# Two late second-layer tiles in halves, other PSUM banks for the last results, and the last inverse deviations one by one

## The chip, the cores and the metric

The kernel runs on one core of one Trainium2 chip. The metric is the device time of one execution in microseconds, as the median of several runs. A core has five engines that work side by side, each through its own list of instructions in order: TensorE (PE, matmuls and transposes), VectorE (DVE), ScalarE (ACT), GpSimd (POOL), and SyncE (SP), which here only issues DMAs. An instruction that waits holds up everything behind it on its own engine.

## The reference

Two stages. A retention layer without a softmax (8 batches, 8 heads, 576 positions, 64 wide), and a feed-forward layer over its 4608 rows of 512:

```python
scores = (q @ k.T) / 8 * gamma_h ** (i - j)      # for i >= j, else 0; one gamma per head
x = concat_heads(scores @ v)                     # 4608 x 512
h = x @ w_in                                     # 4608 x 1024
e = exp(h - max(h)); sm = e / sum(e)
u = h * sm
ln = (u - mean(u)) / sqrt(var(u) + 1e-6) * g_ln
out = ln @ w_out                                 # 4608 x 512
```

## The kernel before

The 4608 rows are 36 tiles of 128, and two neighbouring tiles form a window of 256 positions. The retention part is also cut into 36 steps (a window times four heads, two steps to a window). The program is one list per engine, written out by hand in `ORDER` (lines 53 to 110): each engine runs its names in that order. A planner (`plan`, `order_ops`) only merges the five lists into one order in which tiles are handed out; it moves nothing within an engine. The names, with a number for the tile or the step:

- SP: `ldq`, `ldk`, `ldv` load the inputs (one DMA each, four for the steps 16, 17, 34 and 35); `lx` is a DMA transpose of a tile's product (L568); `out` stores a result.
- POOL: `sq`, `sk`, `cv` scale and cast q, k and v; `sm`, `sc` carry the state between windows; `rs` works out the inverse deviations of both tiles of a window (`rstd`, L770: an addition, then a power, on 128x2).
- TensorE: `T` transposes q and k (L519), `S` scores (L620), `I` and `V` the retention output (L580), `K` the state; `M1` is the first layer of a tile (L713: 8 matmuls into the two banks of "h"), `M2` the second (L786: 8 matmuls of 128x128 by 128x512 into one bank). `L35` is the one late transpose that TensorE makes (L531). The last tile's second layer is cut into two halves of columns, `M2_35` and `M3`.
- ACT: `Te` copies the transposed q and k out of the bank (L550), `xe` the retention output (L702), `ex` is the exponential with its sum (L721), `va` the sum of squares of some tiles (L750), `fx` squares the sums (L759), `Le` copies L's result (L548), `oe` scales a tile's result by its inverse deviation on the way out of PSUM (L795; `oz` for M3).
- DVE: `mask` applies the decay mask (L656), `so` the product h*e (L736, L731), `bnA` and `bnB` the statistics of its halves (L742, with an aggregate, L744), `fin` the deviation's argument for tiles with `va`; `cnt`, `cs`, `ci` count the rows whose sums are in range.

For a tile t the chain is: M1 (bank "h"), ex, so, then lx (or L), then M2 six tiles behind, then oe and out. M1 of the next tile needs "h" back, so it waits for so. M2 waits for the transposed product and for a bank; oe waits for M2 and for rs of its window.

PSUM has eight banks: "xy", "s" and "h" of two banks each with one tile in flight, and "tl" with two banks for the transposes of q and k. Once the last of these has been copied out, "tl" is closed and its two banks become the pool "o2", two tiles of one bank (`bank`, L488). Which pool a tile's M2 writes to is said by `home` (L136); the constant `OT` is the first tile in "o2". Scores use "s" as well, so an M2 in "s" stands between two steps' scores, and the next score waits until oe has emptied it. Results in SBUF ("osb") have three buffers.

The end of TensorE's list before, and those of ACT and SP:

```python
PE:  ... V33 T35 S34 M1_31 M2_27 I34 V34 S35 M1_32 M2_28 I35 V35 M1_33 M2_29 M2_30 M1_34 M2_31 M2_32 M1_35 M2_33 L35 cs M2_34 M2_35 M3
ACT: ... oe26 Te35 xe33 ex31 oe27 xe34 ex32 fx14 oe28 va31 fx15 ex33 va30 xe35 oe30 ex34 oe29 fx16 oe31 ex35 oe32 fx17 oe33 Le35 oe34 oe35 oz
SP:  ... ldk35 lx26 ldq35 out23 lx27 out24 ldv34 lx28 ldv35 out25 lx29 lx30 out27 out26 lx31 lx32 out28 lx33 out30 out29 lx34 out31 ...
```

Of the kernel before, what the change touches and what calls it, by code (L numbers as in the profile page):

```python
# [13 lines left out]
P = 128  # L14
# [3 lines left out]
for _b in range(0, B, 4):  # L18
# [25 lines left out]
R0 = 9  # L44
OT = 30
SPL = ()
# [7 lines left out]
    PE=(  # L54
# [10 lines left out]
    ),  # L65
    ACT=(
# [9 lines left out]
    ),  # L76
    DVE=(
# [9 lines left out]
    ),  # L87
# [9 lines left out]
    ),  # L97
# [38 lines left out]
def home(t):  # L136
    return "h" if t == NT - 1 else "o2" if t >= OT else "xy" if late(t) and t % 2 else "s"


def late(t):  # L140
    return t + LAG >= 37
# [7 lines left out]
def plan():  # L149
# [49 lines left out]
    for t in range(NT):  # L199
# [11 lines left out]
        if c:  # L211
            op(f"fx{w}", "ACT", "fx", [f"ex{t - 1}", f"ex{t}"], (m + 1, 2.6))
            if va:
                op(f"fin{w}", "DVE", "fin", [f"fx{w}", f"va{t - 1}", f"va{t}"], (m + 1, 4.3))
            op(f"rs{w}", "POOL", "rs" if va else "rsB", [f"fin{w}"] if va else [f"fx{w}", f"bnB{t - 1}", f"bnB{t}"], (m + 2, 0.0))
        jn = ev_L(t)[:2] == "TL"
        early = t < NJ - 4
        if t in LX:
            op(f"lx{t}", "SP", "lx", [f"so{t}"], (m + 2, 0.1), [("evl", [f"M2_{t}"])], DUR["ltx"])
        lasts = [x for x in range(NT) if NJ - 4 <= x < OT and ev_L(x)[:2] == "Le"]  # L220
# [10 lines left out]
        if t == OT:  # L231
            need += [ev_T(max(x for x in range(NS) if x not in TX)), ev_L(max(x for x in range(OT) if x not in LX))]
        op(f"M2_{t}", "PE", "M2h" if end else "M2", need, (t + LAG, 3.1), [(home(t), [f"oe{t}"])])
        op(f"oe{t}", "ACT", "oeh" if end else "oe", [f"M2_{t}", f"rs{w}"], (t + LAG + 1, 0.1), [("osb", [f"out{t}"])])
        if end:
# [143 lines left out]
def kernel(  # L379
# [381 lines left out]
    def final(w):  # L761
        d = ws[w]
        d["x2"] = pools["sml"].tile([P, 2], FP, tag="w2", name="w2")
        for c in range(2):
# [3 lines left out]
            )  # L768

    def rstd(w):  # L770
        d = ws[w]
        if 2 * w not in VA:
            d["x2"] = pools["sml"].tile([P, 2], FP, tag="w2", name="w2")
            nc.gpsimd.tensor_tensor(out=d["x2"], in0=d["mv"][:, :, 1], in1=d["x"], op=ALU.add)
        d["rs"] = pools["sml"].tile([P, 2], FP, tag="rs", name="rs")
        nc.gpsimd.tensor_tensor(out=d["rs"], in0=d["x2"], in1=small[:, 69:70].to_broadcast([P, 2]), op=ALU.pow)  # L776


    def mm2(t, half=0):
        d = tk[t]  # L780
        nm = "xy" if half else home(t)
        mm = slice(256 * half, 256 * half + (256 if t == NT - 1 else DM))
        o = bank() if nm == "o2" else pools[nm].tile([P, 2, 512], FP, tag=nm, name="o_ps")[:, 0]
        d["o", half] = o = o[:, 0 : mm.stop - mm.start]
        for c in range(8):
            nc.tensor.matmul(  # L786
                out=o, lhsT=d["ev"][:, d["lo"] + c], rhs=w2c16[:, c, mm], start=(c == 0), stop=(c == 7)
            )

    def o_ev(t, half=0):  # L790
        d = tk[t]
        if not half:
            d["osb"] = pools["osb"].tile([P, DM], FP, tag="osb", name="o_sb")
        mm = slice(256 * half, 256 * half + (256 if t == NT - 1 else DM))
        nc.scalar.activation(  # L795
            out=d["osb"][:, mm], in_=d["o", half], func=ACT.Copy, scale=ws[t // 2]["rs"][:, t % 2 : t % 2 + 1]
        )
# [77 lines left out]
    def emit(o):  # L875
# [39 lines left out]
        elif k_ == "cs":  # L915
            count_b()
        elif k_ == "ci":
            nc.vector.tensor_copy(out=count, in_=cur["cs"][0:1, 0:1])
        elif name[:2] == "wi":
            w_in_cast(int(name[2]), name[3] == "b", copy)  # L920
        else:
            dict(
                T=qk_tp, L=ln_tp, K=kv_mm, I=inter, st=state, sc=state_cast, sm=state_next, S=scores, mask=mask, V=av, xe=x_ev, M1_=mm1,
                ex=exp_, so=solu, va=squares, fx=sums2, fin=final, rs=rstd, M2_=mm2, oe=o_ev, out=store, wc=w2_center,
                M=lambda _: mm2(NT - 1, 1), oz=lambda _: o_ev(NT - 1, 1), G=lambda _: g_tp(), WM=lambda _: w2_sum(), wm=lambda _: w2_mean(),
            )[k_](x)
# [155 lines left out]
```

## Time and profile before

| | us |
|---|---|
| median of three runs | 210.21 (209.46 to 211.24) |
| the profiled execution, its own time | 208.5 |
| its span, first to last instruction | 206.7 |
| TensorE busy in the span | 195.5 |
| DVE busy | 151.4 |
| ACT busy | 140.7 |
| POOL busy | 140.2 |

The profile is one execution on the chip. A row of its timeline gives the start in the span, the length, the engine, the line of the kernel, the operation, the tile written and those read, and how many instructions were merged; in brackets stands how long the engine was idle before it and what ended that. A matmul's row is longer than its share of the engine, since matmuls overlap: the distance from one start to the next tells what a group costs. The granted clock of TensorE is 1.000 over the span. The DMA engines' busy share is over nine tenths in many of the slices up to three quarters of the span, and varies behind that.

### The profile page before, as it was taken

How to read it: one execution, taken by the hardware profiler on the slowest of the kernel's cores; microseconds unless marked ns; L12 is line 12 of the kernel's file. 1: busy time of each engine (PE TensorE's matmuls, PEld its weight loads, DVE VectorE, ACT ScalarE, POOL GpSimd, SP SyncE). 2: the span in 40 equal slices, each digit the busy share in tenths (PEclk: the TensorE clock that was granted, in tenths of full speed). 3: DMA queues.
4: the chain of work that ended last, by engine and by line, in shares of the span. 5: the costliest groups of instructions: out<-in, count | busy, mean ns of one | idle time of the engine just before them, and what ended most of it. 6: DMA issues, size and time to landing. Idle time of an engine off the chain costs nothing. (4 is left out here: it accounts for less than half of the span.)

```text
span 206.7 us, 8546 instructions
## 1 busy us (share of the span) xinstructions
PE 195.5 (95%) x3576; PEld 108.3 (52%) x3576; DVE 151.4 (73%) x269; ACT 140.7 (68%) x250; POOL 140.2 (68%) x235
## 2 busy tenths in 40 slices
PE   7996989999999999999999999999999999999981
PEld 2442654665665555555555555565555555544450
DVE  6575779995988878688897857896878685725850
ACT  2375798897776667667866687696868756576451
POOL 7434758999997797987678888789795853121110
PEclk9999999999999999999999999999999999999999
DMA  6999999999977869999999999999989557998734
GB/s 175 344 358 331 327 318 292 294 263 290 244 220 222 248 197 306 228 284 219 265 291 174 221 296 239 217 255 227 326 132 280 124 117 201 165 236 212 115 149 103
DMA packets 91112, 49.12 MB, mean 238 GB/s; under 512 B 29624, under 2 KB 84928, under 8 KB 91072
## 3 DMA queue, kind: packets, MB, share of 16 engines
q1 hardware_dynamic: 90832, 48.38, 96.3%
q8 instruction: 28, 0.46, 1.0%
q10 hardware_dynamic: 240, 0.18, 0.4%
q14 instruction: 12, 0.10, 0.2%
HBM read 32.56 MB, written 9.44 MB: 203 GB/s over the span
## 5 line engine op out<-in xcount | busy, mean ns | idle before, releaser
L713 PE MATMUL h_ps<-w_in,xT 128*128 128x512 f16 x288 | 68.4, 380 | 0.2 <-DVE solu L736 0.2
L786 PE MATMUL o_ps<-w2c,ev 128*128 128x512 f16 (+1 forms) x296 | 67.6, 373 | 0.0
L721 ACT ACTIVATE e_sb<-h_ps 128x1024 f32<-128x1024 f32 x36 | 36.8, 1022 | 23.7 <-PE h_ps L713 17.3
L656 DVE TENSOR_TENSOR ret<-s_ps,masks 128x1024 f16<-128x1024 f32 x36 | 43.9, 1219 | 11.2 <-PE s_ps L620 10.7
L786 PEld LDWEIGHTS <-ev 128*128 128x128 f16 x296 | 28.9, 98 | 33.0
L713 PEld LDWEIGHTS <-xT 128*128 128x128 f16 x288 | 25.4, 98 | 29.3 <-ACT xT L702 0.7
L477 POOL TENSOR_TENSOR q<-rawq,small 128x512 f16<-128x512 f32 x34 | 35.3, 1042 | 7.3 <-DMA rawq<-in_q_dram 6.6
L736 DVE TENSOR_TENSOR solu<-h_ps,e_sb 128x1024 f16<-128x1024 f32 x22 | 26.9, 1224 | 18.0 <-ACT e_sb L721 17.8
L477 POOL TENSOR_TENSOR k<-rawk,small 128x512 f16<-128x512 f32 x34 | 35.3, 1042 | 6.3 <-DMA rawk<-in_k_dram 5.9
L795 ACT ACTIVATE o_sb<-o_ps,rs 128x512 f32<-128x512 f32 (+1 forms) x37 | 25.0, 675 | 19.3 <-PE o_ps L786 7.7
L742 DVE BATCH_NORM_STATS2 bs<-solu 128x6 f32<-128x512 f16 x44 | 29.8, 681 | 0.1
L702 ACT CAST xT<-xy 128x512 f16<-128x512 f32 x36 | 26.5, 736 | 2.8 <-PE xy L580 2.7
L697 POOL CAST sbd<-gg 64x256 f16<-64x256 f32 x64 | 25.4, 397 | 2.5
L482 POOL CAST v<-rawv 128x512 f16<-128x512 f32 x28 | 17.0, 610 | 9.9 <-DMA rawv<-in_v_dram 3.9
L731 DVE SCALAR_TENSOR_TENSOR solu<-h_ps,e_sb 128x1024 f16<-128x1024 f32 x14 | 17.1, 1221 | 5.7 <-ACT e_sb L721 5.6
L550 ACT COPY ev<-tl 128x512 f32<-128x512 f32 (+1 forms) x26 | 17.8, 684 | 2.0 <-PE tl L519 1.8
L688 POOL TENSOR_TENSOR gg<-gt,small 128x128 f32<-128x128 f32 x32 | 13.1, 408 | 7.9 <-DVE gt L683 7.5
L776 POOL TENSOR_TENSOR rs<-w,small 128x2 f32<-128x2 f32 x18 | 12.4, 690 | 8.5 <-DVE w L765 7.5
L750 ACT ACTIVATE junk<-solu,su 128x1024 bf16<-128x1024 f16 x14 | 16.1, 1150 | 0.0
L620 PE MATMUL s_ps<-ev 64*64 64x128 f16 x576 | 15.1, 220 | 0.4 <-ACT o_sb L795 0.2
L580 PE MATMUL xy<-ret,v 64*64 64x128 f16 x576 | 14.9, 220 | 0.0
L580 PEld LDWEIGHTS <-sbd 128*128 128x128 f16 x128 | 9.4, 98 | 9.4 <-issue 1.1
(73 smaller groups left out, 204.6 us busy)
## 6 DMA issues: line engine op xcount, KB each, us to landing
rawq<-in_q_dram SPq DMA_DIRECT2D x32, 256.0 KB, 5.0
rawk<-in_k_dram SPq DMA_DIRECT2D x32, 256.0 KB, 5.5
rawv<-in_v_dram SPq DMA_DIRECT2D x32, 256.0 KB, 5.1
out_dram<-o_sb SPq DMA_DIRECT2D x32, 256.0 KB, 3.6
wst<-in_moe_w_in_dram SPq DMA_DIRECT2D x4, 512.0 KB, 6.9
wst<-in_moe_w_out_dram SPq DMA_DIRECT2D x4, 512.0 KB, 7.4
rawk<-in_k_dram SPq DMA_DIRECT2D x16, 64.0 KB, 3.4
rawv<-in_v_dram SPq DMA_DIRECT2D x16, 64.0 KB, 3.5
```

The source lines that it names most:

```text
L477: eng.tensor_tensor(out=t.rearrange("p j h d -> p h j d"), in0=st[i]["r" + nm], in1=g, op=ALU.mult)
L550: nc.scalar.copy(out=t[:, lo:hi].rearrange("p x (r w) -> p r x w", r=2), in_=tls[n].rearrange("p r x w -> p (r x w)").bitcast(FP).rearrang ...
L580: nc.tensor.matmul(start=(c, e) not in begun, stop=False, skip_group_check=True, **kw)
L656: nc.vector.tensor_tensor(out=d["ret"].rearrange("p e h j q -> p (e h) (j q)")[:, :, 0:n], in0=d["s"].rearrange("p e h j q -> p (e h) (j q ...
L697: nc.gpsimd.tensor_copy(out=t[ee[e], :, :, ee[e]], in_=st[i]["gg"][ee[e]])
L702: nc.scalar.copy(out=xT[:, 2 * w : 2 * w + 2, 2 * hf : 2 * hf + 2].rearrange("p c h (q j) -> p c h j q", j=2), in_=xys[i][:, :, 0:256].rea ...
L713: nc.tensor.matmul(out=h_ps[:, hh], lhsT=xT[:, t, dc], rhs=w_in16[:, dc, hh], start=(dc == 0), stop=(dc == 3),)
L721: nc.scalar.activation(out=d["e"], in_=d["h"], func=ACT.Exp, accum_out=se[:, t : t + 1])
L736: nc.vector.tensor_tensor(out=d["solu"], in0=d["h"], in1=d["e"], op=ALU.mult)
L742: nc.vector.bn_stats(out=d["bs"][:, half], in_=d["solu"][:, half * 512 : half * 512 + 512])
L786: nc.tensor.matmul(out=o, lhsT=d["ev"][:, d["lo"] + c], rhs=w2c16[:, c, mm], start=(c == 0), stop=(c == 7))
L795: nc.scalar.activation(out=d["osb"][:, mm], in_=d["o", half], func=ACT.Copy, scale=ws[t // 2]["rs"][:, t % 2 : t % 2 + 1])
```

## The change

- `CUT = (29, 32)`: the second layer of tiles 29 and 32 is issued in two groups of four matmuls, `M2_t` and `N_t`, into one accumulation. The first layer of tiles 33 and 35 stands between them. oe and the buffer of the transposed product now wait for `N_t`.
- Banks: `OT` goes from 30 to 27, so the M2 of tiles 27 to 30, 32 and 33 write to "o2"; those of 31 and 34 write to "s". Before, tiles up to 29 were in "s" and 30 to 34 in "o2". The last tile stays in "h".
- The last window's inverse deviations are worked out one tile at a time: `ra` for tile 34 from its own statistics, then `rs17` for tile 35, each on 128x1. oe34 waits for `ra`.
- Orders: on ACT va31 goes ahead of ex32, xe35 ahead of ex33, and oe29 and oe30 change places. On DVE bnB32 goes ahead of so34. On POOL `ra` comes ahead of rs17. On SP ldq35 goes ahead of lx26, and out30 behind out29 and lx34.

```diff
-OT = 30
+OT = 27
+CUT = (29, 32)
...
-PE:  ... I35 V35 M1_33 M2_29 M2_30 M1_34 M2_31 M2_32 M1_35 M2_33 L35 cs M2_34 M2_35 M3
+PE:  ... I35 V35 M2_29 M1_33 N29 M2_30 M1_34 M2_31 M2_32 M1_35 N32 M2_33 L35 cs M2_34 M2_35 M3
-ACT: ... xe34 ex32 fx14 oe28 va31 fx15 ex33 va30 xe35 oe30 ex34 oe29 fx16 oe31 ex35 ...
+ACT: ... xe34 va31 ex32 fx14 oe28 xe35 fx15 ex33 va30 oe29 ex34 oe30 fx16 oe31 ex35 ...
-DVE: ... so33 bnA32 fin15 bnA33 so34 bnB32 bnB33 bnA34 ...
+DVE: ... so33 bnA32 fin15 bnA33 bnB32 so34 bnB33 bnA34 ...
-POOL: ... rs14 rs15 rs16 rs17
+POOL: ... rs14 rs15 rs16 ra rs17
-SP:  ... ldk35 lx26 ldq35 out23 ... out28 lx33 out30 out29 lx34 out31 ...
+SP:  ... ldk35 ldq35 lx26 out23 ... out28 lx33 out29 lx34 out30 out31 ...
...
-    return "h" if t == NT - 1 else "o2" if t >= OT else "xy" if late(t) and t % 2 else "s"
+    return "h" if t == NT - 1 else "s" if t in (NT - 5, NT - 2) else "o2" if t >= OT else "xy" if late(t) and t % 2 else "s"
...
+    def rstd_of(c):
+        d = ws[NW - 1]
+        y = pools["sml"].tile([P, 1], FP, tag=f"wy{c}", name="w2")
+        nc.gpsimd.tensor_tensor(out=y, in0=d["mv"][:, c, 1:2], in1=d["x"][:, c : c + 1], op=ALU.add)
+        d["rs", c] = pools["sml"].tile([P, 1], FP, tag=f"rs{c}", name="rs")
+        nc.gpsimd.tensor_tensor(out=d["rs", c], in0=y, in1=small[:, 69:70], op=ALU.pow)
...
-        for c in range(8):
+        for c in range(4 if t in CUT else 8):
             nc.tensor.matmul(
                 out=o, lhsT=d["ev"][:, d["lo"] + c], rhs=w2c16[:, c, mm], start=(c == 0), stop=(c == 7)
             )
+
+    def mm2_rest(t):
+        d = tk[t]
+        for c in range(4, 8):
+            nc.tensor.matmul(
+                out=d["o", 0], lhsT=d["ev"][:, d["lo"] + c], rhs=w2c16[:, c], start=False, stop=(c == 7)
+            )
```

(The five order lists are shown by their ends, one line each; in the kernel they are strings over several lines.)

More of the change, by code (lines that the diff above doesn't have):

```diff
@@ L54 @@
     PE=(
[10 rows of a table removed]
+        "G T0 S0 K0 K1 T1 I0 S1 V0 I1 V1 M1_0 K2 T2 T3 K3 S2 M1_1 I2 S3 V2 L0 I3 V3 T4 L1 K4 S4 M1_2 K6 WM K5 M1_3 T5 K7  T6 I4 S5 V4 T7 I5 S6 V5 T8 M1_4 I6 S7 V6 K8 T9 L2 M2_0 I7 L3 V7 K9 S8 M1_5 M2_1 I8 L4 T10 V8 S9 K10 M1_6 M2_2  I9 V9 L5 T11 S10 K11 M1_7 M2_3 I10 V10 L6 T12 K12 S11 M1_8 M2_4 I11 V11 L7 T13 K13 S12 M1_9 M2_5 I12 V12 L8 T14  K14 S13 M1_10 M2_6 I13 V13 L9 T15 K15 S14 M1_11 M2_7 I14 V14 T16 S15 M1_12 M2_8 I15 V15 T17 S16 M1_13 M2_9 I16  V16 T18 K18 S17 M1_14 M2_10 I17 T19 V17 K19 S18 M1_15 M2_11 I18 V18 K20 T20 S19 M1_16 M2_12 I19 V19 K21 T21 S20  M1_17 M2_13 I20 V20 T22 K22 S21 M1_18 M2_14 I21 V21 K23 T23 S22 M1_19 M2_15 I22 T24 V22 K24 S23 M1_20 M2_16 I23  V23 K25 T25 S24 M1_21 M2_17 I24 V24 K26 T26 S25 M1_22 M2_18 I25 V25 K27 T27 S26 M1_23 M2_19 I26 V26 K28 T28 S27  M1_24 M2_20 I27 T29 V27 K29 S28 M1_25 M2_21 I28 V28 T30 K30 S29 M1_26 M2_22 I29 T31 V29 K31 S30 M1_27 M2_23 I30  V30 K32 T32 S31 M1_28 M2_24 I31 V31 T33 K33 S32 M1_29 M2_25 I32 T34 V32 S33 M1_30 M2_26 I33 V33 T35 S34 M1_31  M2_27 I34 V34 S35 M1_32 M2_28 I35 V35 M2_29 M1_33 N29 M2_30 M1_34 M2_31 M2_32 M1_35 N32 M2_33 L35 cs M2_34 M2_35 M3"
@@ L65 @@
     ),
     ACT=(
[9 rows of a table removed]
+        "cv0 cv1 Te0 Te1 wi2a wi1a xe0 wi0a wi3a xe1 cv2 ex0 Te2 cv3 Te3 wg4 wg0 ex1 xe2 cv4 Le0 xe3 Te4 Le1 wg6 wg2 cv6  ex2 cv5 va1 cv7 ex3 Te5 va2 Te6 xe4 fx1 fx0 Te7 xe5 va0 Te8 ex4 xe6 Le2 va3 oe0 xe7 Le3 Te9 ex5 oe1 TL8 xe8 ex6  oe2 TL9 xe9 ex7 oe3 xe10 TL10 fx2 ex8 oe4 TL11 xe11 ex9 oe5 fx3 xe12 TL12 fx4 ex10 oe6 xe13 TL13 ex11 oe7 xe14  Te16 ex12 oe8 xe15 Te17 fx5 ex13 oe9 Te18 xe16 ex14 fx6 oe10 va14 xe17 ex15 Te19 oe11 fx7 va15 xe18 ex16 Te20  oe12 xe19 Te21 ex17 oe13 fx8 xe20 Te22 ex18 oe14 xe21 Te23 ex19 oe15 Te24 xe22 va19 ex20 oe16 xe23 Te25 va18  ex21 fx9 oe17 fx10 xe24 Te26 ex22 oe18 xe25 Te27 va22 ex23 fx11 oe19 Te28 xe26 ex24 oe20 va23 xe27 ex25 Te29  oe21 fx12 Te30 xe28 ex26 oe22 Te31 xe29 va26 ex27 oe23 Te32 xe30 ex28 fx13 oe24 va27 xe31 Te33 ex29 oe25 xe32  ex30 Te34 oe26 Te35 xe33 ex31 oe27 xe34 va31 ex32 fx14 oe28 xe35 fx15 ex33 va30 oe29 ex34 oe30 fx16 oe31 ex35  oe32 fx17 oe33 Le35 oe34 oe35 oz"
@@ L76 @@
     ),
     DVE=(
[9 rows of a table removed]
+        "gc sq0 sq1 st0 mask0 st1 wi1b mask1 wi2b wi3b wi0b sk2 sk3 st2 so0 st3 wg5 mask2 mask3 so1 st4 wg7 wg1 wg3  mask4 st6 so2 st5 wc4 wc0 wc7 wc1 st7 so3 mask5 wc5 wc2 wc6 mask6 wc3 mask7 fin0 st8 so4 mask8 st9 bnA4 so5  fin1 bnA5 mask9 st10 bnB4 so6 bnB5 mask10 st11 bnA6 so7 bnA7 mask11 st12 bnB7 so8 bnA8 mask12 st13 bnB6 so9  bnB8 mask13 st14 so10 bnA9 mask14 bnB9 st15 so11 bnA10 mask15 so12 bnA11 mask16 bnB11 bnB10 so13 mask17 st18  bnA13 so14 bnA12 mask18 st19 bnB13 so15 mask19 bnB12 st20 fin7 so16 bnA16 mask20 st21 bnB16 so17 mask21 st22  so18 bnA17 mask22 bnB17 st23 so19 mask23 st24 so20 mask24 bnA20 st25 so21 fin9 mask25 st26 bnB20 so22 bnA21  mask26 st27 bnB21 so23 mask27 st28 so24 bnA24 mask28 bnB24 st29 fin11 so25 mask29 bnA25 st30 so26 mask30 st31  bnB25 so27 mask31 st32 so28 mask32 st33 bnA28 so29 fin13 mask33 bnA29 so30 mask34 bnB29 so31 mask35 bnB28 so32  so33 bnA32 fin15 bnA33 bnB32 so34 bnB33 bnA34 bnB34 so35 cnt bnA35 bnB35 ci"
@@ L214, in plan @@
                 op(f"fin{w}", "DVE", "fin", [f"fx{w}", f"va{t - 1}", f"va{t}"], (m + 1, 4.3))
+            if w == NW - 1:
+                op("ra", "POOL", "rsB", [f"fx{w}", f"bnB{t - 1}"], (m + 2, 0.0))
             op(f"rs{w}", "POOL", "rs" if va else "rsB", [f"fin{w}"] if va else [f"fx{w}", f"bnB{t - 1}", f"bnB{t}"], (m + 2, 0.0))
@@ L218, in plan @@
         if t in LX:
-            op(f"lx{t}", "SP", "lx", [f"so{t}"], (m + 2, 0.1), [("evl", [f"M2_{t}"])], DUR["ltx"])
+            op(f"lx{t}", "SP", "lx", [f"so{t}"], (m + 2, 0.1), [("evl", [f"N{t}" if t in CUT else f"M2_{t}"])], DUR["ltx"])
         lasts = [x for x in range(NT) if NJ - 4 <= x < OT and ev_L(x)[:2] == "Le"]
@@ L232, in plan @@
             need += [ev_T(max(x for x in range(NS) if x not in TX)), ev_L(max(x for x in range(OT) if x not in LX))]
-        op(f"M2_{t}", "PE", "M2h" if end else "M2", need, (t + LAG, 3.1), [(home(t), [f"oe{t}"])])
-        op(f"oe{t}", "ACT", "oeh" if end else "oe", [f"M2_{t}", f"rs{w}"], (t + LAG + 1, 0.1), [("osb", [f"out{t}"])])
+        cut = t in CUT
+        op(f"M2_{t}", "PE", "M2h" if end or cut else "M2", need, (t + LAG, 3.1), [(home(t), [f"oe{t}"])])
+        if cut:
+            op(f"N{t}", "PE", "M2h", [f"M2_{t}"], (t + LAG, 4.0))
+        op(f"oe{t}", "ACT", "oeh" if end else "oe", [f"N{t}" if cut else f"M2_{t}", "ra" if t == NT - 2 else f"rs{w}"], (t + LAG + 1, 0.1), [("osb", [f"out{t}"])])
         if end:
@@ L768, in final @@
             )
+    def rstd_of(c):
[4 more added lines that the diff above has]
+        nc.gpsimd.tensor_tensor(out=d["rs", c], in0=y, in1=small[:, 69:70], op=ALU.pow)
     def rstd(w):
         d = ws[w]
+        if w == NW - 1:
+            return rstd_of(1)
         if 2 * w not in VA:
@@ L795, in o_ev @@
         nc.scalar.activation(
-            out=d["osb"][:, mm], in_=d["o", half], func=ACT.Copy, scale=ws[t // 2]["rs"][:, t % 2 : t % 2 + 1]
+            out=d["osb"][:, mm], in_=d["o", half], func=ACT.Copy,
+            scale=ws[t // 2]["rs", t % 2] if t // 2 == NW - 1 else ws[t // 2]["rs"][:, t % 2 : t % 2 + 1],
         )
@@ L924, in emit @@
                 ex=exp_, so=solu, va=squares, fx=sums2, fin=final, rs=rstd, M2_=mm2, oe=o_ev, out=store, wc=w2_center,
-                M=lambda _: mm2(NT - 1, 1), oz=lambda _: o_ev(NT - 1, 1), G=lambda _: g_tp(), WM=lambda _: w2_sum(), wm=lambda _: w2_mean(),
+                M=lambda _: mm2(NT - 1, 1), N=mm2_rest, ra=lambda _: rstd_of(0), oz=lambda _: o_ev(NT - 1, 1), G=lambda _: g_tp(), WM=lambda _: w2_sum(), wm=lambda _: w2_mean(),
             )[k_](x)
```

34 rows, old and new, of tables (ACT, DVE, PE, POOL) are left out of this document.

## The prediction

> **What bounds the kernel now.** I read the page first (busy shares), then TensorE's timeline over the last 40 us for its idle time, then the SP queue and the landing of its DMAs, then ACT and DVE around each gap.
>
> ```profile
> span 206.7 us, 8546 instructions
> ## 1 busy us (share of the span) xinstructions
> PE 195.5 (95%) x3576; PEld 108.3 (52%) x3576; DVE 151.4 (73%) x269; ACT 140.7 (68%) x250; POOL 140.2 (68%) x235
> ```
>
> TensorE is busy for 95% of the span. Whatever the change can win is idle time of TensorE, and the diff only touches the last eight tiles. So the whole possible gain is in the gaps that the timeline shows there:
>
> ```profile
> 170.61 1.89 PE L786 MATMUL o_ps<-w2c,ev 128*128 128x512 f16 x8
> ...
> 173.36 0.32 PE L519 MATMUL tl<-ident,q 64*64 64x64 f16 x16 [0.29 <-POOL q L477]
> ...
> 173.67 0.42 PE L620 MATMUL s_ps<-ev 64*64 64x128 f16 x16
> ...
> 178.42 0.42 PE L620 MATMUL s_ps<-ev 64*64 64x128 f16 x16 [0.20 <-ACT o_sb L795]
> ```
>
> By the order list these are M2_26 (170.61), T35 (0.29 idle, waiting for sq35 on POOL), S34, and S35 (0.20 idle, waiting for oe27 to free the bank "s"). Then the end:
>
> ```profile
> 183.13 1.89 PE L713 MATMUL h_ps<-w_in,xT 128*128 128x512 f16 x8 [0.15 <-DVE solu L736]
> 184.86 3.62 PE L786 MATMUL o_ps<-w2c,ev 128*128 128x512 f16 x16
> 188.31 1.89 PE L713 MATMUL h_ps<-w_in,xT 128*128 128x512 f16 x8
> 190.04 3.62 PE L786 MATMUL o_ps<-w2c,ev 128*128 128x512 f16 x16
> 193.49 1.89 PE L713 MATMUL h_ps<-w_in,xT 128*128 128x512 f16 x8
> 195.22 1.89 PE L786 MATMUL o_ps<-w2c,ev 128*128 128x512 f16 x8
> 197.85 0.62 PE L531 MATMUL o_ps<-ident,solu 128*128 128x128 f16 x8 [0.74 <-ACT o_sb L795]
> 198.40 0.19 PE L873 MATMUL cs<-small,cn 128*1 128x1 f32 x2
> 198.52 3.65 PE L786 MATMUL o_ps<-w2c,ev 128*128 128x512 f16 x24
> ```
>
> These are M1_33, M2_29 with M2_30, M1_34, M2_31 with M2_32, M1_35, M2_33, L35, cs, and M2_34, M2_35 and M3. A group of eight matmuls takes 1.73 us from start to start (193.49 to 195.22), four take 0.865. The reader should see two kinds of stretch. Between M1_33 and M1_34 there are three groups (5.18 us) and no gap: TensorE is the bound. Between M1_35 and L35 there are only two (3.46), and L35 comes 4.36 after M1_35 started. That 4.36 is a chain through other engines: exp on ACT, the product on DVE, then the next user of the bank "h" or of the product. It is the least distance of one first-layer tile from the next. So the end is a PE-bound part with surplus work between two tiles, followed by a chain-bound part with too little.
>
> **The change part by part.**
>
> 1. *Two groups.* M2_29 and M2_32 are cut in halves: the first half of M2_29 goes ahead of M1_33, the second behind it, and likewise around M1_35. From the start of M1_33 to L35, TensorE then has 3 first-layer tiles (5.19), halves of M2_29, M2_32 and again M2_32 (2.60) and M2_30, M2_31, M2_33 (5.19): 12.98 us, with 2.6 us between any two tiles. The chain needs 3 x 4.36 = 13.08. The two nearly meet, and I take the longer. Before it was 197.85 - 183.13 = 14.72. That is 1.64 less, but half a tile (0.865) now stands ahead of M1_33: 0.77 gained. The 0.15 before M1_33 goes too, as M2_29 fills it. The number of matmuls is the same, and a group that pauses keeps its bank, so I put nothing on the cut; were each cut to cost one matmul more (0.22), it would be 0.4.
>
> 2. *Banks.* M2_27 to M2_29 move from "s" to the pair "o2"; M2_31 and M2_34 move from "o2" to "s". S35 no longer waits for oe27: 0.20 gained. M2_34 no longer waits for oe33. The price: M2_27 is now the first to take the banks of "tl", free when Te35 has read them. Its row is the copy on ACT just behind oe26:
>
> ```profile
> 172.93 0.69 ACT L795 ACTIVATE o_sb<-o_ps,rs 128x512 f32<-128x512 f32 x1 [0.53 <-DMA out_dram<-o_sb]
> ...
> 178.28 0.73 ACT L702 CAST xT<-xy 128x512 f16<-128x512 f32 x1
> 180.71 1.02 ACT L721 ACTIVATE e_sb<-h_ps 128x1024 f32<-128x1024 f32 x1 [1.70 <-DVE bs L742]
> ...
> 183.57 1.14 ACT L750 ACTIVATE junk<-solu,su 128x1024 bf16<-128x1024 f16 x1
> ...
> 200.69 1.16 ACT L795 ACTIVATE o_sb<-o_ps,rs 128x512 f32<-128x512 f32 x2 [1.61 <-POOL rs L776]
> 202.26 0.47 ACT L795 ACTIVATE o_sb<-o_ps,rs 128x256 f32<-128x256 f32 x1 [0.41 <-PEq L1037]
> ```
>
> oe26 ends at 173.62 and Te35 follows within a microsecond, while M2_27 comes a whole first-layer tile (1.73) after S34's end: hidden.
>
> 3. *ACT.* va31 (1.14, the size of va30's row at 183.57) moves into the 1.70 of idle time before ex32 (180.71), behind xe34 (178.28): hidden; without that room it would delay ex32 and so M1_33 by what sticks out. xe35 goes ahead of ex33, which waits for M1_33 anyway. oe29 and oe30 change places to follow the order of M2.
>
> 4. *DVE.* bnB32 goes ahead of so34.
>
> ```profile
> 181.85 1.23 DVE L736 TENSOR_TENSOR solu<-h_ps,e_sb 128x1024 f16<-128x1024 f32 x1 [0.90 <-ACT e_sb L721]
> 186.20 1.22 DVE L736 TENSOR_TENSOR solu<-h_ps,e_sb 128x1024 f16<-128x1024 f32 x1 [3.12 <-ACT e_sb L721]
> 187.34 0.68 DVE L742 BATCH_NORM_STATS2 bs<-solu 128x6 f32<-128x512 f16 x1
> ```
>
> Between the end of one product and the start of the next there are 4.36 - 1.22 = 3.14 us. It now holds three statistics (3 x 0.68), fin15 and an aggregate; if the last two take as long as one statistic together, that is 2.7, and 0.4 is left. If they took double, so34 would be 0.3 late, and with it L35. I take nothing.
>
> 5. *POOL, last inverse deviations.* Tile 34's is worked out by itself (ra) before tile 35's. The rows at 200.69 and 202.26 show what this is worth: oe34 waited for POOL until 200.69, though M2_34 ended near 200.4, but the last output oz waits for M3 (198.52 + 3.65 = 202.17), not for oe34. So it gains nothing at the end, and out34 leaves some 0.3 sooner. Two small POOL operations more cost at most the same 0.4 that oz has to spare.
>
> 6. *SP queue.* This is the part that speaks against the change. ldq35 (four issues) now goes ahead of lx26, the DMA transpose that M2_26 reads.
>
> ```profile
> 166.12 1.23 SPq L568 DMA_TRANSPOSE ev<-solu  x1
> 167.45 1.96 SPq L467 DMA_DIRECT2D rawq<-in_q_dram  x4
> 169.51 1.32 SPq L806 DMA_DIRECT2D out_dram<-o_sb  x1
> ...
> 179.50 2.65 SPq L568 DMA_TRANSPOSE ev<-solu  x2
> ```
>
> lx26 went out at 166.12. Behind four loads that hold the queue from 167.45 to 169.51 (2.06) it goes out at 168.18. From issue to landing, the last ten transposes (from 161 us on, so far as the trace holds their landing) took, as minimum, median and maximum:
>
> ```profile
> DMA to landing us min/median/max: 3.1/3.5/4.1
> ```
>
> So lx26 lands at 171.28, 171.68 or 172.28, and M2_26, which started at 170.61 with no wait, is late by 0.67, 1.07 or 1.67. Behind it on TensorE stand I33, V33, T35, S34, M1_31. Of this, 0.29 comes back at T35: ldq35 leaves 1.33 sooner, so sq35 is there first. The rest, 0.38, 0.78 or 1.38, stays in TensorE's order. oe26 is 0.69 long and follows M2_26, so S34 (three small stages later) finds its bank free. Loads, lx27 and all later ones keep their places: the two exchanged lengths cancel.
>
> 7. *M2_29 earlier.* It could start at 182.98 (the end of V35: 183.13 less 0.15) less 0.20 for S35 = 182.78, plus the delay of step 6: 183.16, 183.56 or 184.16. But lx29, the first of the pair at 179.50, has this row of its own:
>
> ```profile
> DMA to landing us min/median/max: 4.1/4.1/4.1
> ```
>
> It lands at 183.6. Before, M2_29 came at 184.86 and did not see it; now it does. M2_29 starts at the later of the two: 183.6 in the low and middle cases, 184.16 in the high one. This wait therefore hides most of what step 6 does.
>
> *Later transposes.* lx33 and lx34 leave when so33 and so34 are done. M2_34 comes 4.36 + 0.67 after so34, above the 4.1 maximum, so nothing.
>
> *Sum.* L35 starts at M2_29 + 0.865 + 13.08 = 183.6 + 13.945 = 197.55, against 197.85. Everything behind L35 (M2_34, M2_35, M3, oz, out35) keeps its distances. The span is 0.30 shorter: 206.4. That execution took 208.5 beside its span of 206.7, so the sum is 208.2 against 208.5. It was quicker than all three runs (median 210.21), so I carry over the difference, not the level: 209.9.
>
> **The rivals.**
>
> *All gaps close (faster).* If lx26 and lx29 land in time, M2_29 starts at 182.78, L35 at 196.73, 1.12 earlier: 209.1. It needs lx26 within 2.4 us of its issue (170.61 - 168.18) and lx29 within 3.3 (182.78 - 179.50); no transpose in the window was under 3.1. [...]
>
> *A late transpose decides (slower).* One mechanism: lx26 behind the loads. Break-even is M2_29 at 197.85 - 13.945 = 183.91, which is lx26 landing 3.85 us after its issue. All 25 transposes of the trace spread further than the last ten:
>
> ```profile
> DMA to landing us min/median/max: 3.1/4.2/6.6
> ```
>
> At their median of 4.2, M2_26 is 1.77 late, M2_29 starts at 184.26, and the kernel is 0.35 slower: 210.6. At 6.6 it is 2.75 slower: 213.0. For it: lx26 now stands behind eight loads in a row (ldk35's four and ldq35's). Against: it stood behind ldk35's four before, and the last ten transposes kept within 4.1.
>
> *It does nothing at the end.* If a link of the chain is longer than 4.36 in the new order (step 4, or the cut), L35 keeps its 197.85 whatever happens ahead of it: 210.2.
>
> **How the numbers follow.** 0.56 for the forecast (M2_29 between 183.16 and 184.16: 209.5 to 210.5), 0.14 for all gaps closing, 0.24 for a late transpose (about 0.04 of it beyond 2.1 us), 0.06 for nothing at the end. No case reaches 1% faster (2.1 us), as all the gaps that are touched sum to 1.12 once the half tile is paid; 1% is about what a measurement of this kernel can tell from no change, as its three runs alone spread from 209.46 to 211.24. For that spread I leave 0.06 to faster and 0.06 to slower, 0.88 to within 1%. The range takes the fast rival's 209.1 and the slow one's 210.6, and widens each by 0.4 and 0.8, the first for the spread of a median, the second also for the tail towards 213: 208.7 to 211.4.
>
> **What would show it.** In the trace after: M2_26 with an idle time of 0.7 to 1.7 before it; no idle time before T35 and S35; M2_29's first four matmuls waiting for a transpose until about 183.6; M1_33 to L35 in 13.1 us instead of 14.72; L35 with little idle time before it; oe34 not waiting for POOL. It is wrong if M2_26 does not wait (step 6), if M1_33 to L35 stays above 13.6 (step 1), or if something outside these eight tiles moves.

## The result, and the profile after

| | us |
|---|---|
| kernel before, median of 15 runs | 209.52 (208.59 to 211.24) |
| changed kernel, median of 15 runs | 207.95 (206.86 to 210.28) |
| ratio of the two kernels' runs (their medians alone give 0.9925) | 0.993, 95% interval 0.9905 to 0.9956 |
| profiled execution of the changed kernel, its own time and span | 209.56 and 207.8 |

The change makes the kernel faster by 0.7% (0.9 to 2.0 us). It is within 1%, as forecast, but outside the range of 208.7 to 211.4, and five times the 0.3 us forecast. The profile that came with it shows the opposite at first sight: its span is longer than that of before.

```profile
span 207.8 us, 8550 instructions
## 1 busy us (share of the span) xinstructions
PE 196.0 (94%) x3576; PEld 108.1 (52%) x3576; DVE 152.1 (73%) x269; ACT 139.9 (67%) x250; POOL 140.9 (68%) x237
```

So this execution is one of the slowest of the fifteen (only one run, 210.28, which the ratio leaves out, took longer than its 209.56), while the profiled one of before, at 208.5, was under the fastest of its fifteen (208.59). TensorE's timeline of the changed kernel, from M2_26 on:

```profile
173.07 1.90 PE L776 MATMUL o_ps<-w2c,ev 128*128 128x512 f16 x8 [1.34 <-DMA ev<-solu]
174.81 0.39 PE L561 MATMUL xy<-ev,sbd 128*128 128x128 f16 x4
175.13 0.42 PE L561 MATMUL xy<-ret,v 64*64 64x128 f16 x16
175.38 0.29 PE L500 MATMUL tl<-ident,q 64*64 64x64 f16 x16
...
179.94 0.42 PE L561 MATMUL xy<-ret,v 64*64 64x128 f16 x16
180.19 0.39 PE L601 MATMUL s_ps<-ev 64*64 64x128 f16 x16
...
184.65 1.04 PE L776 MATMUL o_ps<-w2c,ev 128*128 128x512 f16 x4
185.53 1.89 PE L694 MATMUL h_ps<-w_in,xT 128*128 128x512 f16 x8
...
198.58 0.62 PE L512 MATMUL o_ps<-ident,solu 128*128 128x128 f16 x8
199.13 0.19 PE L871 MATMUL cs<-small,cn 128*1 128x1 f32 x2
199.25 1.90 PE L776 MATMUL o_ps<-w2c,ev 128*128 128x512 f16 x8
201.45 1.92 PE L776 MATMUL o_ps<-w2c,ev 128*128 128x256 f16 x16 [0.30 <-ACT ev L529]
```

M2_26 is idle for 1.34 us, waiting for its transpose (step 6). T35 and S35 no longer wait. From M1_33 (185.53) to L35 (198.58) it takes 13.05 us instead of 14.72, as step 1 worked out (13.08). New is the last row: M2_35 waits 0.30 for Le35. ACT's timeline shows why:

```profile
200.24 0.69 ACT L792 ACTIVATE o_sb<-o_ps,rs 128x512 f32<-128x512 f32 x1 [2.30 <-DMA out_dram<-o_sb]
200.82 0.58 ACT L529 COPY ev<-o_ps 128x512 f32<-128x512 f32 x1
```

The first is oe33. It waits for the landing of out30 (issued at 195.5, landed 4.6 us later), whose buffer in SBUF it reuses (three buffers), and Le35 stands behind it on ACT.

### The profile page after: what moved, and what is told of

The parts are those of the page before. It is cut to its first block, busy times and chain, and to the rows that moved or that the text cites. A ratio compares the mean times of both kernels' runs of the same rounds, so it can differ in the third digit from the quotient of the medians.

```text
span 207.8 us, 8550 instructions
## 1 busy us (share of the span) xinstructions
PE 196.0 (94%) x3576; PEld 108.1 (52%) x3576; DVE 152.1 (73%) x269; ACT 139.9 (67%) x250; POOL 140.9 (68%) x237
## 5 line engine op out<-in xcount | busy, mean ns | idle before, releaser
L776 PE MATMUL o_ps<-w2c,ev 128*128 128x512 f16 (+1 forms) x288 | 66.2, 373 | 1.6 <-DMA ev<-solu 1.3
L776 PEld LDWEIGHTS <-ev 128*128 128x128 f16 x288 | 27.8, 98 | 34.0 <-DMA ev<-solu 1.8
L766 POOL TENSOR_TENSOR rs<-w,small 128x2 f32<-128x2 f32 x17 | 11.7, 691 | 8.9 <-DVE w L746 7.9
L969 PE MATMUL tl<-zeros 128*128 128x512 f16 x41 | 13.1, 455 | 1.3 <-DVE zeros L932 1.3
```

What stands on the lines that cost most here:

```text
L776: nc.tensor.matmul(out=o, lhsT=d["ev"][:, d["lo"] + c], rhs=w2c16[:, c, mm], start=(c == 0), stop=(c == 7))
```

## The experiments

Between one profile and the next the start of M1_30 moves by up to 2 us (168.87 before, 170.77 in E4) for reasons far ahead of the change: in the first profile of the changed kernel M1_12 already starts 1.02 later than in that of the kernel before (83.61 against 82.59), and M1_30 0.97 later. So each profile below is read from there: the distance from M1_30's start to L35's, and from L35 to the end of the last matmul. "lx26 ahead" is the time from the issue of lx26 to M1_30's start; M2_26 can start 1.74 after M1_30 (170.61 and 168.87 before, where it did not wait).

| kernel | ratio to before (interval) | M1_30 to L35 | L35 to last matmul's end | lx26 ahead |
|---|---|---|---|---|
| before | 1 | 28.98 | 4.31 | 2.75 |
| before, again (E10) | one run | 29.08 | 4.32 | 2.70 |
| changed | 0.993 (0.9905 to 0.9956) | 28.74 | 4.80 | 1.34 |
| changed, again (E11) | one run | 27.24 | 4.56 | 4.10 |
| E1 changed, lx26 ahead of ldq35 | 0.9923 (0.9895 to 0.9952) | 27.24 | 4.31 | 4.78 |
| E2 before, ldq35 first | 0.9973 (0.9951 to 0.9995) | 28.63 | 4.32 | 2.69 |
| E3 before, new banks | 0.997 (0.9944 to 0.9996) | 28.24 | 4.32 | 5.26 |
| E4 changed, cut undone | 0.9951 (0.9931 to 0.9971) | 29.87 | 4.32 | 1.42 |
| E5 changed, lx26 ahead of ldk35 | 0.9925 (0.9897 to 0.9954) | 27.29 | 4.61 | 6.66 |
| E6 changed, paired deviations | 0.993 (0.9902 to 0.9957) | 27.44 | 4.54 | 1.77 |
| E7 changed, out30 ahead of lx34 | 0.9933 (0.9912 to 0.9955) | 27.24 | 4.32 | 3.69 |
| E8 changed, old banks | 1.0066 (1.0035 to 1.0097) | 28.67 | 5.67 | 2.54 |
| E9 lx26 first and out30 early | 0.9912 (0.9877 to 0.9946) | 27.62 | 4.31 | 6.18 |
| E12 lx26 between, out30 early | 0.994 (0.9917 to 0.9962) | 27.23 | 4.32 | 5.95 |

**E1, the order of lx26 and ldq35 undone in the changed kernel.**

```diff
-... ldk35 ldq35 lx26 out23 ...
+... ldk35 lx26 ldq35 out23 ...
```

> The changed kernel with one thing undone: lx26 goes ahead of ldq35 again. Theory 1 (the gaps close as worked out and the lateness of lx26 is usually hidden or small): M2_26 no longer waits, T35 waits some 0.3 us again, and the time stays within 0.3 us of the changed kernel, ratio to before 0.990 to 0.995. Theory 2 (lx26's lateness costs TensorE about 1 us in most executions): it is 0.5 to 1 us faster than the changed kernel, ratio 0.987 to 0.990. Theory 3 (the early ldq35 is itself the gain that the sum lacked): it is 0.5 to 1 us slower than the changed kernel, ratio 0.996 to 0.998.

Ratio 0.9923, in the range of theory 1. Its interval rules out theory 3 and only just reaches theory 2: the exchange is not what makes the changed kernel faster, and a cost of 0.5 us is not shown either. The profile has no idle time of note from M1_30 to the end. T35 does not wait, though ldq35 is behind lx26 again; there theory 1 was wrong.

**E2, the exchange alone.**

```diff
-... ldk35 lx26 ldq35 out23 ...
+... ldk35 ldq35 lx26 out23 ...
```

> The kernel before with one thing of the change: ldq35 goes ahead of lx26. Theory 1: M2_26 waits and T35 does not, between no change and 0.4 us slower, ratio 1.000 to 1.002. Theory 2: 0.5 to 1 us slower, ratio 1.002 to 1.005. Theory 3: 0.5 to 1 us faster, ratio 0.995 to 0.998.

Ratio 0.9973, under 1 by little more than its interval: faster, where theories 1 and 2 had no change or a loss; theory 3's range holds it, yet E1 speaks against theory 3. M2_26 (170.71, 1.74 after M1_30 at 168.97) did not wait:

```profile
170.71 1.89 PE L786 MATMUL o_ps<-w2c,ev 128*128 128x512 f16 x8
172.44 0.39 PE L580 MATMUL xy<-ev,sbd 128*128 128x128 f16 x4
172.75 0.42 PE L580 MATMUL xy<-ret,v 64*64 64x128 f16 x16
173.00 0.29 PE L519 MATMUL tl<-ident,q 64*64 64x64 f16 x16
```

These rows, of TensorE in E2, also show how a gap is to be read. The last V33 row (172.75) is 0.42 long, yet T35 starts 0.25 after it. In the kernel before, the same two rows were these:

```profile
172.65 0.42 PE L580 MATMUL xy<-ret,v 64*64 64x128 f16 x16
173.36 0.32 PE L519 MATMUL tl<-ident,q 64*64 64x64 f16 x16 [0.29 <-POOL q L477]
```

The idle time shown is 0.29, but from start to start it is 0.71 against 0.25: the wait costs 0.46, of which 0.11 comes back on the way from T35 to S34. A matmul's row is longer than its turn on the engine: where nothing waits, the next row starts before this one has ended (173.00 against 173.17).

**E3, the new banks alone.**

```diff
-OT = 30
+OT = 27
...
-    return "h" if t == NT - 1 else "o2" if t >= OT else "xy" if late(t) and t % 2 else "s"
+    return "h" if t == NT - 1 else "s" if t in (NT - 5, NT - 2) else "o2" if t >= OT else "xy" if late(t) and t % 2 else "s"
```

> The kernel before with the banks of the change alone (M2 of tiles 27 to 29 in o2, of 31 and 34 in s). Theory 1 and 2: S35 no longer waits for oe27, 0.2 to 0.3 us faster, ratio 0.9985 to 0.999. Theory 3: the same. If the banks alone give 0.6 us or more, the wait for oe27 is longer in most executions than in the profiled one.

Ratio 0.997 (0.63 us), two to three times what was expected, though the interval (0.9944 to 0.9996) reaches that too. A longer wait for oe27 in most executions is not what the profiles show: S35 is idle for 0.19 or 0.20 in all four that have the old banks (before, E10, E2, E8). The rows of V34 and S35 in E3:

```profile
179.15 0.42 PE L580 MATMUL xy<-ret,v 64*64 64x128 f16 x16
179.40 0.39 PE L620 MATMUL s_ps<-ev 64*64 64x128 f16 x16
```

From start to start 0.25, against 177.81 to 178.42 (0.61) before. With 0.03 more in the two groups behind, the freed bank is worth 0.39, where the 0.20 of idle time had been read. The rest of E3's shorter M1_30 to L35 (0.74 less than before) is T35, which did not wait in this execution; SP's order is not changed in E3, so that part is not put down to the banks.

**E4, the cut undone.**

```diff
-CUT = (29, 32)
+CUT = ()
...
-... V35 M2_29 M1_33 N29 M2_30 M1_34 M2_31 M2_32 M1_35 N32 M2_33 ...
+... V35 M1_33 M2_29 M2_30 M1_34 M2_31 M2_32 M1_35 M2_33 ...
```

> The changed kernel with the second layer of tiles 29 and 32 in one group each, behind M1_33 and ahead of M1_35 as before. Theory 1: from M1_33 to L35 takes 14.7 us again, and 0.8 to 0.9 us are lost against the changed kernel, ratio 0.996 to 0.998. Theory 2: the same loss. Theory 3 (the gain lies in the early load): it keeps 0.8 us or more of the gain, ratio 0.994 to 0.996.

Ratio 0.9951 (0.9931 to 0.9971): it falls in theory 3's range, and its interval reaches into that of theories 1 and 2. The loss against the changed kernel is 0.4 us and not 0.8 to 0.9, but the intervals of the two overlap, so its size is not shown by these times. A reason for less than 0.8 is below: what the cut gains at L35 it partly gives back behind it. The profile is of the longest of the thirteen runs (211.20), so its length proves nothing, but its distances show two things. These are TensorE's rows of M1_30, M2_26, M1_33 and L35, and SP's of lx26:

```profile
170.77 1.90 PE L694 MATMUL h_ps<-w_in,xT 128*128 128x512 f16 x8
174.12 1.90 PE L776 MATMUL o_ps<-w2c,ev 128*128 128x512 f16 x8 [1.46 <-DMA ev<-solu]
...
185.93 1.89 PE L694 MATMUL h_ps<-w_in,xT 128*128 128x512 f16 x8 [0.15 <-DVE solu L717]
...
200.64 0.62 PE L512 MATMUL o_ps<-ident,solu 128*128 128x128 f16 x8 [0.74 <-DVE solu L717]
```

```profile
169.35 1.23 SPq L549 DMA_TRANSPOSE ev<-solu  x1
```

First, from M1_33 to L35 it takes 14.71 us, as theory 1 had it and as before the change (14.72), against 13.05 with the cut. L35's idle time of 0.74, which its row before put down to ACT, is here put down to the product on DVE, 4.36 after M1_35: that is the chain of the prediction. Second, M2_26 waits again: lx26 left only 1.42 ahead of M1_30.

**E5, lx26 ahead of both groups of loads.**

```diff
-... lx25 ldk35 ldq35 lx26 out23 ...
+... lx25 lx26 ldk35 ldq35 out23 ...
```

> The changed kernel with lx26 ahead of both ldk35 and ldq35 on SP, so that eight loads no longer stand before it. Theory A (M2_26 waits in some executions only because the queue reaches lx26 too late): lx26 lands over 1 us before M1_30 has ended, M2_26 never waits, M1_30 to M1_33 takes 14.2 us as in the variant with lx26 ahead of ldq35 (before: 14.26 without the half tile of 0.87 in between), and the time is 0.4 to 0.8 us under the changed kernel's, ratio 0.989 to 0.992. Theory B (the wait comes from the transposes themselves being slow at that place): M2_26 still waits now and then and the ratio stays at 0.993.

In the profile M2_26 does not wait, as theory A had it, but the ratio of 0.9925 is not apart from 0.993. The runs here range only from 207.12 to 207.93, against 206.86 to 210.28 of the changed kernel; with nine runs that is a hint and no more.

**E6, the deviations in a pair.**

```diff
-... rs16 ra rs17
+... rs16 rs17
...
-            scale=ws[t // 2]["rs", t % 2] if t // 2 == NW - 1 else ws[t // 2]["rs"][:, t % 2 : t % 2 + 1],
+            scale=ws[t // 2]["rs"][:, t % 2 : t % 2 + 1],
```

> The changed kernel with the last two inverse deviations in one pair again. Theory A: oe34 waits for POOL again, but the last output waits for M3, so no change: from L35 to the end of TensorE's last matmul 4.3 us (4.8 where Le35 is late), ratio within 0.001 of the changed kernel's. Theory B (the separate deviation is worth something): 0.3 us slower, ratio 0.9945.

Ratio 0.993, the same as with them apart, so theory A holds. ACT's timeline of E6 has oe33 waiting for out30, then Le35, then oe34 waiting for POOL, and the last output well after that:

```profile
198.45 0.69 ACT L788 ACTIVATE o_sb<-o_ps,rs 128x512 f32<-128x512 f32 x1 [2.04 <-DMA out_dram<-o_sb]
199.03 0.58 ACT L527 COPY ev<-o_ps 128x512 f32<-128x512 f32 x1
199.90 0.69 ACT L788 ACTIVATE o_sb<-o_ps,rs 128x512 f32<-128x512 f32 x1 [0.29 <-POOL rs L762]
200.80 0.47 ACT L788 ACTIVATE o_sb<-o_ps,rs 128x256 f32<-128x256 f32 x1 [0.21 <-PE o_ps L772]
201.68 0.47 ACT L788 ACTIVATE o_sb<-o_ps,rs 128x256 f32<-128x256 f32 x1 [0.41 <-PEq L1031]
```

The 0.29 before oe34 is covered by the 0.21 and 0.41 behind it, in which ACT waits for TensorE.

**E7, out30 ahead of lx34.**

```diff
-... lx33 out29 lx34 out30 out31 ...
+... lx33 out29 out30 lx34 out31 ...
```

> The changed kernel with out30 issued ahead of lx34. In the profile of the changed kernel oe33 waited until 200.24 for the landing of out30, and behind it on ACT Le35, and M2_35 came 0.30 late. Theory A: out30 now lands some 3 us sooner, oe33 follows M2_33 at once, L35 to the last matmul takes 4.31 us, and M2_34 still finds lx34 landed: 0.3 to 0.5 us faster than the changed kernel, ratio 0.991 to 0.992. Theory B: lx34 now waits for oe30 and lands too late for M2_34: slower by up to 1 us, ratio 0.994 to 0.998.

The profile shows theory A: L35 to the last matmul's end is 4.32 again, and oe33 waits for M2_33 alone, as ACT's row says:

```profile
196.21 0.69 ACT L792 ACTIVATE o_sb<-o_ps,rs 128x512 f32<-128x512 f32 x1 [0.80 <-PE o_ps L776]
196.79 0.58 ACT L529 COPY ev<-o_ps 128x512 f32<-128x512 f32 x1
```

The ratio of 0.9933 does not show the 0.25 to 0.5 us; it lies within the interval of the changed kernel, so a gain in the time is not shown.

**E8, the cut with the old banks.**

```diff
-OT = 27
+OT = 30
...
-    return "h" if t == NT - 1 else "s" if t in (NT - 5, NT - 2) else "o2" if t >= OT else "xy" if late(t) and t % 2 else "s"
+    return "h" if t == NT - 1 else "o2" if t >= OT else "xy" if late(t) and t % 2 else "s"
```

> The changed kernel with the banks of before (M2 of tiles 27 to 29 in s, 30 to 34 in o2). Theory A: S35 waits for oe27 (0.36 us by distance of starts, 0.20 by the idle time shown), and M2_29, now ahead of M1_33, waits for oe28 to empty the bank, which ends about 1 us after V35: 1.2 to 1.6 us slower than the changed kernel, ratio 0.9985 to 1.001. Theory B (the banks matter by the wait for oe27 alone): 0.2 to 0.4 us slower, ratio 0.994 to 0.995.

Ratio 1.0066: slower than before, and by more than theory A's range. TensorE's rows with a wait in E8:

```profile
178.87 0.42 PE L601 MATMUL s_ps<-ev 64*64 64x128 f16 x16 [0.20 <-ACT o_sb L792]
...
184.24 1.02 PE L776 MATMUL o_ps<-w2c,ev 128*128 128x512 f16 x4 [0.81 <-ACT o_sb L792]
...
200.36 3.63 PE L776 MATMUL o_ps<-w2c,ev 128*128 128x512 f16 x24 [1.29 <-ACT o_sb L792]
```

S35 and M2_29 wait as expected. The third wait was not foreseen: M2_34, in "o2" again, waits for oe33, which in the changed kernel, with the same order of stores, waited 2.30 us for out30. So the new order needs the new banks in two places: the cut needs them at M2_29, and the late out30 at M2_34. In the kernel before, with the same banks and out30 earlier, M2_34 did not wait (198.52, 0.12 behind cs).

**E9, lx26 first and out30 early.** The diffs of E5 and E7 together.

> The changed kernel with both mended places: lx26 ahead of ldk35 and ldq35, out30 ahead of lx34. Theory A (these two waits are what is left): no wait before M2_26 and none before M2_35, M1_30 to L35 27.25 us and L35 to the last matmul 4.31; 0.3 to 0.6 us under the changed kernel in the median, ratio 0.990 to 0.9925. Theory B (the waits are seldom there): the ratio stays at 0.993.

Ratio 0.9912, in theory A's range, but the interval holds theory B's 0.993 as well. Neither M2_26 nor M2_35 waits, and L35 to the end takes 4.31; but T35 waits 0.24 for POOL here, since ldq35 now comes last of the three. That and a start of M2_29 0.14 late make M1_30 to L35 27.62 and not 27.25. What lx26 gains, ldq35 can lose.

**E10 and E11, both kernels again.**

> The kernel before, for a second profile. If the first profile was of an execution whose SP queue was late (ldk35 held it for 3.41 us, against 1.95 to 1.98 in five variants, and 2.66 where lx26 stands ahead of it), then ldk35 takes about 2 us here, T35 does not wait, M1_30 to M1_33 takes 13.9 us instead of 14.26, and M1_33 to L35 14.7 again. If the late queue is the rule for this order, it is 14.2 to 14.3 again.

> The changed kernel, for a second profile. Theory A: M2_26 waits in some executions only, for 0 to 1.5 us as SP reaches lx26 (a landing before the end of M1_30 needs its issue 1.4 us or more ahead of M1_30's start, as in the two variants where ldq35 stands ahead and nothing waited: 2.7 and 3.7 ahead). M1_30 to M1_33 is 14.2 us plus that wait. Theory B: 1.3 us again, as in the first profile.

E10's SP queue and T35, E10 being the kernel before:

```profile
163.44 3.05 SPq L467 DMA_DIRECT2D rawk<-in_k_dram  x4
166.58 1.23 SPq L568 DMA_TRANSPOSE ev<-solu  x1
167.91 1.96 SPq L467 DMA_DIRECT2D rawq<-in_q_dram  x4
```

```profile
173.87 0.32 PE L519 MATMUL tl<-ident,q 64*64 64x64 f16 x16 [0.39 <-POOL q L477]
```

ldk35 holds the queue for 3.05 us again and T35 waits again, so the expectation that the first profile was an exception is not borne out; but in E1, E3 and E12, with the same order here, ldk35 took 1.96 to 1.98 and T35 did not wait. In E11, the changed kernel, the same stretch of SP and TensorE reads:

```profile
164.47 1.80 SPq L448 DMA_DIRECT2D rawq<-in_q_dram  x4
166.37 1.92 SPq L549 DMA_TRANSPOSE ev<-solu  x1
```

```profile
170.47 1.90 PE L694 MATMUL h_ps<-w_in,xT 128*128 128x512 f16 x8
172.21 1.89 PE L776 MATMUL o_ps<-w2c,ev 128*128 128x512 f16 x8
```

lx26 goes out 4.10 us ahead of M1_30, lands 3.8 after its issue, and M2_26 starts without a wait. In the first profile it went out 1.34 ahead (168.50 against 169.84) and took 4.5 to land:

```profile
168.50 1.23 SPq L549 DMA_TRANSPOSE ev<-solu  x1
```

```profile
DMA to landing us min/median/max: 4.5/4.5/4.5
```

So theory A holds: the wait is there in some executions. Of the seven profiles in the table with ldk35 and ldq35 both ahead of lx26 (the changed kernel twice, E2, E4, E6, E7, E8), two have it, the changed kernel's first and E4, and in these two lx26 left latest (1.34 and 1.42 ahead). The landing counts as much as the issue: with the 3.1 us of E6, where lx26 left 1.77 ahead and M2_26 did not wait, the transpose of the first profile would have landed at 171.60, when M2_26 could start (171.58).

**E12, SP's old order at lx26, out30 early.** The diffs of E1 and E7 together.

> The changed kernel with SP's order of before around ldk35, lx26, ldq35, and with out30 ahead of lx34. If the gain is the sum of the three closed gaps (V34 to S35 0.39 shorter, V35 to the next group 0.22, M1_33 to L35 0.80 with the half tile counted), with no wait at M2_26 and none at M2_35, then M1_30 to L35 takes 27.24 us (27.6 if T35 waits as in both profiles of the kernel before), L35 to the last matmul 4.31, and the ratio is 0.991 to 0.993. If the early ldq35 carries part of the gain (as the kernel before with that alone suggests, ratio 0.997), T35 waits here and the ratio is 0.994 to 0.996.

The profile is as the sum of the three gaps has it (27.23 and 4.32, span 204.9), and T35 does not wait. The ratio of 0.994 lies in the range that was given for a T35 that waits, so profile and time do not point the same way. The ratio is not apart from that of the changed kernel, nor from those of E1, E5, E7 or E9: no variant is shown to beat it.

## Why the prediction was wrong

*The account of the gain.* From M1_30 to the last matmul's end, the kernel before takes 33.29 and 33.40 us in its two profiles, the changed kernel without a wait at M2_26 31.80 (E11): 1.5 to 1.6 us. That is 0.7% of 209.5, as measured, though from single executions. The forecast of 0.30 had the mechanism of the cut, the banks and the deviations right, and failed in these steps:

1. *Steps 6 and 7, positions taken from one execution.* They set lx26 at 168.18, 0.69 ahead of M1_30, and lx29's landing at 183.6, 14.7 after it, and held both as fixed. In the seven profiles with that order lx26 went out 1.34 to 4.10 ahead, and M2_26 waited in two. So the forecast put as the rule a lateness that two of seven show; by its own sign (M2_26 does not wait) step 6 was wrong in five. The place came from a profile in which ldk35 held the queue for 3.41 us; in all seven it held it for 1.95 to 1.97. lx29 hardly mattered: by the distance from V35, M2_29 came 0.21 late in E6 and 0.14 in E9, and not late in either profile of the changed kernel. This is the step that turned the sum from 1.12 to 0.30.

2. *Step 2 and the "all gaps close" rival, sizes read from idle time.* Measured from start to start, the gap at S35 was worth 0.39 and not 0.20, that at M1_33 0.22 (0.57 to 0.35) and not 0.15. T35's wait was used only to take up lateness, but closes as well: V33 to S34 takes 0.67 instead of 1.01 and 1.12, so 0.34 to 0.45. With 0.80 at the end this gives 1.75 to 1.86, against the 1.74 and 1.84 by which E11 is shorter from M1_30 to L35. The rival's 1.12 left out 0.6 of it, and its condition on lx26, a landing within 2.4 us, was not needed once lx26 goes out sooner.

3. *"Everything behind L35 keeps its distances".* It does not: moving out30 behind lx34 was given no price of its own. out30's landing holds oe33, and Le35 behind it, and the stretch behind L35 is longer for it by 0.49 us in the changed kernel's first profile, 0.25 in E11, 0.23 in E6 and 0.30 in E5, though not in E1. E7 takes that away in the profile. In E4, without the cut, the same late out30 costs nothing (4.32). So the cut is worth 0.22 + 0.80 less 0.23 to 0.49 where oe33 is late, some 0.5 to 0.8 us, which fits E4 better than the 0.8 to 0.9 expected there.

Right were step 1 (13.08 worked out, 13.05 and 13.06 measured, and 14.71 where E4 undoes the cut), steps 3 and 4 (no product or exponential came late) and step 5 (E6). In the first profile the wait at M2_26, 1.34 of idle time and 1.49 by the starts, lies in the forecast band of 0.67 to 1.67, but by luck: lx26 left 0.65 sooner than worked out (1.34 ahead and not 0.69), and it took 4.5 us to land, above the 4.1 that was the maximum of the sum. The chance for a change within 1% was right too.

The range failed by 0.75 us, and 0.69 of that is its level: it stood on 210.21, the median of three runs, where fifteen gave 209.52. As a difference its low end, the rival's 1.12 with 0.4 for spread, reached to 1.5 us faster, and 1.57 was measured by the medians. That it came so near is no merit of the sum, which had 0.30.

The rival in which all gaps close came nearer in its outcome, 209.1, than the forecast, but not by the quick landing that it asked for: lx26 took 4.5 and 3.8 us to land in the two profiles of the changed kernel, not 2.4, and in the second it was in time because it left sooner. These rows of the kernel before give the median from issue to landing of loads, stores and transposes of one size (the 128x1024 of a transpose in two bytes are 256 KB too):

```profile
rawq<-in_q_dram SPq DMA_DIRECT2D x32, 256.0 KB, 5.0
rawk<-in_k_dram SPq DMA_DIRECT2D x32, 256.0 KB, 5.5
rawv<-in_v_dram SPq DMA_DIRECT2D x32, 256.0 KB, 5.1
out_dram<-o_sb SPq DMA_DIRECT2D x32, 256.0 KB, 3.6
...
ev<-solu SPq DMA_TRANSPOSE x25, 4.2
```

The transposes' 4.2 lies between the stores' 3.6 and the loads' 5.0 to 5.5. So by these medians the transposes landed no later after their issue than loads of that size, and all of them are above the 2.4 that the rival asked for.

*Open.* Why ldk35 holds the queue for under 2 us in one execution and over 3 in another, and so how often lx26 is late or T35 waits, was not settled. Both profiles of the kernel before have the long ldk35, none of the three variants with that order (E1, E3, E12) does; whether that is chance can't be told from five profiles. Of the 1.74 and 1.84, T35's part is 0.34 to 0.45; without it the change would be worth some 0.9 to 1.2 us (0.39 + 0.22 + 0.80, less 0.25 to 0.49), and the measured 0.9 to 2.0 holds that as well. E2's 0.3% is the size of T35's wait (0.34 to 0.45 us), which fits, but shows it only if that wait is the rule in the kernel before.

## What to carry to other kernels

Read the cost of a gap in TensorE from start to start against the same pair of rows where nothing waits, not from the idle time beside it (0.46 and 0.29 us at T35). A DMA's place in one profile is a sample (lx26 left 1.34 to 4.10 us ahead of M1_30 in the seven profiles that have it behind ldk35 and ldq35): before a lateness is put into a sum, take a second profile, or price it with a chance. And when the order of stores changes, follow the buffers that they free as far as the next engine's list; three buffers reach from an early store to a copy on the last chain (out30 to Le35, and 0.30 us of idle time at M2_35).

## What the runs showed of the hardware

A group of 16 matmuls of 64x64 by 64x128 has a row 0.42 us long, but the next group starts 0.25 us after it when nothing waits (E2, 172.75 to 173.00). ldk35's four loads held the SP queue for 1.95 us (E2, E4, E11) to 3.41 us (before; E10: 3.05) with nothing changed in them. lx26, a DMA transpose of 128x1024, landed 3.1 us (before, E6) to 4.5 us (the changed kernel's first profile) after its issue.
